# Feeding a recurrent attention loop by blocks: per-block rows instead of a resident copy, and second buffers for what is stored

## The chip, the cores and the metric

The kernel runs on one core of one Trainium2 chip. The time is device microseconds of one execution. Five engines work side by side and meet through semaphores: PE (TensorE: matrix products and transposes, into PSUM), DVE (VectorE), ACT (ScalarE), POOL (GpSimd) and SP (SyncE), which in this kernel issues every DMA, one after the other in one queue.

## What is computed

The reference is one layer's output and all its gradients. The layer adds to x a recurrent attention with memory and a dense block, both of the normalized x:

```python
def _A_ref(x, mem0, Wq, Wk, Wv, Wo, seg_len):          # x 1 x 2048 x 512, 32 heads of 128, seg_len 32
    mem = mem0                                          # 8 rows
    for s in range(n_seg):                              # 64 segments
        h = jnp.concatenate([mem, x[:, s*seg_len:(s+1)*seg_len]], axis=1)      # 40 rows
        q, k, v = (jnp.einsum('btd,dhe->bhte', h, W) for W in (Wq, Wk, Wv))
        p = _softmax(jnp.where(mask, jnp.einsum('bhqe,bhke->bhqk', q, k) * scale, -1e9))
        o = jnp.einsum('bhte,hed->btd', jnp.einsum('bhqk,bhke->bhqe', p, v), Wo)
        mem = o[:, :M]                                  # the first 8 rows go to the next segment
        outs.append(o[:, M:])
# out = x + _A_ref(xn, ...) + w2 @ relu(w1 xn + b1)**2 + b2 ; then the vjp by grad_out
```

What matters is that segment s + 1 can't begin before the eight memory rows of segment s are there.

## The kernel before

The program has seven stages, one after the other.

**Stage 1** (lines 181 to 329) works in four pieces of 512 rows: `norm` normalizes x, turns it on PE and keeps the result as `HT` (128 x 4 x 2048, channels on the partitions, all rows on the free axis). Then come the dense block forward and backward. Two "jobs" per 128 rows, 32 in this stage, turn weights for later: `wturn` reads a piece of a weight with a DMA transpose into `wtt` (line 245) and, three jobs later, stores it to DRAM as S_WOT or S_WT (line 249). The other 32 jobs are left over for stage 3.

**Stage 2** (331 to 376) forms the dense weights' gradients.

**Stage 3** (379 to 405) projects the rows that wait at the end of each segment. Each segment's window has 40 places, 8 for memory and 32 for its own rows; the kernel lays the sequence out so that a segment's 32 columns of `HT` are 8 memory rows and 24 of its own, and the first 8 of its own rows, which the memory displaces, are the "left" rows. `XL` gathers these from `HT` (line 386, three copies on DVE and one on ACT), 512 columns in all. 48 products `dNL` of 128 rows by 1024 follow, each of eight matrix multiplications (line 396), copied out of PSUM half by ACT and half by DVE (398) into one of six buffers, and stored to S_NL by one DMA (399). Wo, 4 MB, is loaded as the stage begins (382).

**Stage 4** (407 to 884) is the forward recurrence: 64 steps, grouped in 16 blocks of four. A step projects q, k and v from `HT` (427), copies them from PSUM into the tile `N` (411 ACT, 414 DVE; the profile calls it f_N), turns q and k on PE (166) and copies them back, forms scores, softmax, the weighted sums into the block's tile `OT`, gathers them through Wo (468), sums over groups (479, 487), and writes the eight memory rows of the next step into `HT` (414, "HT<-ps_sum"). Three stores save the step for the backward pass: `soN` (861: q and k rows out of N), `soV` (860: v rows out of N), `soP` (862: the probabilities, E). The left rows of block b are worked on during block b + 1, woven into its steps.

The order in this stage is written by hand: `F_ORDER` has one line for each of the four steps of a block, and `play` (582) issues the named pieces in just that order; a trailing "-" takes the piece of the step or block before, a "+" that of the one after, and "L." names left work. So each engine's queue, SP's too, has a fixed order. In it `soV` of the third step stands in the fourth, behind four other transfers of left work, and `soV` of the fourth stands in the next block's first step. `N` has one buffer: the first copy of a step waits until the step before has stored all of it.

`OT` has one buffer as well. When a block is done, `sO` (698) stores it to DRAM as S_OB, and during the next block four DMA transposes `t0` to `t3` (702) read it from there into `OC` (two buffers, one tag with `ON`), which `u0` to `u3` (704) store as S_ON. `otr` (747) turns the left rows' sums, OTL, straight out of SBUF into ON; `lo` (752) stores that. `sx` (761, 762) stores the block's output and its piece of `HT`.

**Stages 5 to 7** go backward over the left rows, backward over the 64 steps, and form the attention weights' gradients from what was stored.

In stages 1 to 3 a scheduler of the language orders each engine's instructions; in stage 4 and in the backward loop the written order stands.

Of the kernel before, what the change touches and what calls it, by code (L numbers as in the profile page):

```python
# [12 lines left out]
P = 128  # L13
# [13 lines left out]
def kernel(  # L27
# [74 lines left out]
    HG = 4  # L102
# [14 lines left out]
    S_HT = dram.tile([P, DC, S], BF16, name="S_HT")  # L117
    S_GM = dram.tile([P, DC, S], BF16, name="S_GM")
# [15 lines left out]
    S_OB = dram.tile([NB, P, HG, KH, P], BF16, name="S_OB")  # L134
# [46 lines left out]
    with sb("p1", 1) as p1, sb("p1b", 2) as p1b:  # L181
# [6 lines left out]
        def norm(rb):  # L188

            x = xq[rb]  # L190
            bs_ = p1b.tile([P, RCB, 6], F32, name="bs_", tag="bs_")
            mv = p1b.tile([P, RCB, 2], F32, name="mv", tag="mv")
            for c in range(RCB):
                nc.vector.bn_stats(bs_[:, c, :], x[:, c, :])
                nc.vector.bn_aggr(mv[:, c, :], bs_[:, c, :])
            veps = p1b.tile([P, RCB], F32, name="veps", tag="veps")
            nc.vector.tensor_scalar(out=veps[:], in0=mv[:, :, 1], scalar1=EPS, scalar2=None, op0=ALU.add)
            nc.scalar.sqrt(veps[:], veps[:])
            nc.vector.reciprocal(rstd_t[:, rb * RCB:(rb + 1) * RCB], veps[:])
            xn = p1b.tile([P, RCB, D], BF16, name="xn", tag="xn")  # L200
            for c in range(RCB):
                nc.vector.tensor_scalar(out=xn[:, c, :], in0=x[:, c, :], scalar1=mv[:, c, 0:1],
                                        scalar2=rstd_t[:, rb * RCB + c:rb * RCB + c + 1], op0=ALU.subtract,
                                        op1=ALU.mult)
# [55 lines left out]
        for rb in range(NRB):  # L260
# [68 lines left out]
        dma(out_8.rearrange("(c p) -> p c", p=P), gb1b[:])  # L329

# [52 lines left out]
    with sb("fl", 2) as fl:  # L383
        XL = fl.tile([P, DC, NB * NL], BF16, name="XL", bufs=1)
        for dc in range(DC):
            nc.any.tensor_copy(XL[:, dc].rearrange("p (s t) -> p s t", t=M),
                               HT[:, dc].rearrange("p (s r) -> p s r", r=SEG)[:, :, 0:M])
        for t in (1, 0, 2):
            for g in range(HG):
                for q in range(NB // 4):  # L390
# [8 lines left out]
                    dma(S_NL[4 * q:4 * q + 4, 32 * g:32 * g + 32, t, :], dN[:])  # L399
# [182 lines left out]
    def play(order, n, steps, lefts, step, blk, last={}):  # L582
# [36 lines left out]
    with sb("fw", 1) as fw, psum("fr", 4) as fr, psum("fpp", 1) as fpp, \  # L619
# [42 lines left out]
        nc.vector.tensor_copy(HT[:, :, 0:M], psm0[:, 0:DC * M].rearrange("p (c m) -> p c m", c=DC))  # L662
# [21 lines left out]
        def left(b):  # L684
# [13 lines left out]
            o["sO"] = lambda: dma(S_OB[b], B_["OT"][:].rearrange("p g k j r -> p g k (j r)"))  # L698
            for g in range(HG):
                def tO(g=g):  # L700
                    st["OC", g] = fo.tile([P, KH, P], BF16, name="OC", tag="OC", bufs=2)
                    nc.sync.dma_start_transpose(st["OC", g][:], S_OB[b][:, g].rearrange("p k r -> p (k r)"))
# [57 lines left out]
            def sx():  # L760
                dma(out0flat[b * P:(b + 1) * P, :], B_["bb"][:])
                dma(S_HT[:, :, b * P:(b + 1) * P], HT[:, :, b * P:(b + 1) * P])
            o["sx"] = sx
            return o

        def fwd(s):
# [3 lines left out]
            hT = HT[:, :, s * SEG:(s + 1) * SEG]  # L770
            shapes = {"kT": (fo, [P, KH, HG, L]), "qT": (fo, [P, KH, HG, SEG]), "N": (fo, [P, 3, GW])}
# [26 lines left out]
            for t, u, n in ((1, 2, "k"), (0, 1, "q"), (2, 0, "v")):  # L798
                for p in range(2):
                    def mm(n=n, p=p, t=t):  # L800
                        ps[n, p] = big("ps_proj")
                        proj(ps[n, p], hT, Wqkv, t * HD, p)
# [51 lines left out]
            def HTf():  # L854
                if s + 1 < NSEG:
                    ENGS["HT"](HT[:, :, (s + 1) * SEG:(s + 1) * SEG + M], st["sum"][:, :, 0:M])
# [11 lines left out]
        def load_back():  # L868
# [5 lines left out]
            dma(back["WoT"][:], S_WOT[:])  # L874
        with tc.manual_schedule():
# [9 lines left out]
    ht_cm.__exit__(None, None, None)  # L885
# [501 lines left out]
```

## Time and profile before

| | |
|---|---|
| median of 3 runs | 3427.52 us (3426.79 to 3429.24) |
| the profiled execution, its span | 3435.4 us |
| PE busy | 2761.0 us, 80% |
| DVE, ACT, POOL busy | 1220.0, 1017.2, 187.6 us |
| packets under 512 B | 650689 of 881602 |
| DMA engines' mean busy share | 74.8% in SP's queue |

The profiled execution's own time is its span, 7.9 us (0.23%) above the median of the runs. In the views, "A <- B" means that A came when B let it; times are microseconds from the start of the span, and "x3" counts instructions that a row merges. A row of SP's queue has how long SP was held by issuing that DMA, not how long the transfer took; a row "DMA a<-b" of the chain of waits has issue to landing. "PEclk" is the granted share of PE's clock.

### The profile page before, as it was taken

Reading aid. Unit: us, or ns where it says so; the run is one execution under the profiler, and the core shown is the slowest. Engines: PE = TensorE matmul, PEld = TensorE weight load, DVE = VectorE, ACT = ScalarE, POOL = GpSimd, SP = SyncE. Lnnn points to the kernel's source line nnn. Section 1 sums busy time; section 2 is a strip of 40 time slices with the busy share of each in tenths; the row PEclk is TensorE's granted clock in tenths of the full one; section 3 lists DMA queues with packets and bytes.
Section 4 is the critical chain, followed back from the end, with each engine's and each line's share of the span. In section 5 each row is a group of like instructions: output and inputs, shape, how many; then the busy total and the mean of one; then the engine's idle time right before and its main releaser. Section 6 shows DMA issues by size and latency. Waiting matters only on the chain.

```text
span 3435.4 us, 115446 instructions
## 1 busy us (share of the span) xinstructions
PE 2761.0 (80%) x51768; PEld 1351.9 (39%) x51768; DVE 1220.0 (36%) x3529; ACT 1017.2 (30%) x2493; POOL 187.6 (5%) x329
## 2 busy tenths in 40 slices
PE   7998854788777888774558888888788865999999
PEld 3453322444344444442233444344344432444444
DVE  5440112555454554542334444344444420010101
ACT  2331111333343343331333334333333320111111
POOL 0000001000000000000000000000000000000000
PEclk9999987999999999996679999999999988999999
DMA  9948997566657656667975767766766779999992
GB/s 259 269 116 333 217 174 132 146 163 168 174 156 181 173 164 181 161 173 220 257 202 151 204 162 181 190 163 171 199 158 172 206 201 224 224 194 226 190 196 77
DMA packets 881602, 644.73 MB, mean 188 GB/s; under 512 B 650689, under 2 KB 737362, under 8 KB 869714
## 3 DMA queue, kind: packets, MB, share of 16 engines
q1 hardware_dynamic: 881106, 637.34, 74.8%
q8 instruction: 406, 6.65, 0.8%
q14 instruction: 90, 0.74, 0.1%
HBM read 224.54 MB, written 264.25 MB: 142 GB/s over the span
## 4 chain that ended last, share of the span: by engine, by line
PE 58%; DMA 16%; SPq 11%; DVE 5%; ACT 5%; issue 4%; ACTq 0%; POOLq 0%; POOL 0%; DVEq 0%
PE ps_gw L1348 15%; PE ps_gR L468 11%; PE ps_proj L427 8%; SPq L245 3%; PE b_pp L553 3%; DMA S_A<-f_N 3%; PE ps_tr L166 3%; DMA S_GOL<-l_gON 3%; PE ps_R L468 3%; DMA ON<-OTL 2%; ACT R L411 2%; PE ps_sum L479 2%; PE ps_RL L1055 1%; PE ps_w L354 1%; DMA b_qN<-S_A 1%
## 5 line engine op out<-in xcount | busy, mean ns | idle before, releaser
L1348 PE MATMUL ps_gw<-gn,HNc 128*128 128x512 bf16 x1920 | 416.4, 379 | 0.0
L427 PE MATMUL ps_proj<-Wqkv,HT 128*32 128x512 bf16 x6144 | 378.8, 398 | 18.2 <-DVE HT L414 17.9
L411 ACT CAST f_N<-ps_proj 128x512 bf16<-128x512 f32 x320 | 182.1, 585 | 376.7 <-DMA S_A<-f_N 197.2
L1348 PEld LDWEIGHTS <-HNc 128*128 128x128 bf16 x1920 | 187.8, 98 | 223.9
L427 PEld LDWEIGHTS <-HT 128*32 128x32 bf16 x6144 | 161.1, 101 | 186.9 <-DVE HT L414 30.0
L1323 ACT CAST wt<-ps_gw 128x512 bf16<-128x512 f32 x126 | 70.7, 589 | 514.2 <-PE ps_gw L1348 291.9
L1306 DVE TENSOR_TENSOR gx<-ps_rows,gb 128x512 f32<-128x512 f32 x16 | 11.1, 692 | 495.7 <-PE ps_rows L1304 465.1
L1348 PE MATMUL ps_gw<-GOc,gn 128*128 128x512 bf16 x640 | 142.8, 386 | 18.9 <-DMA gn<-S_ON 18.9
L468 PE MATMUL ps_gR<-WT,b_gq 128*32 128x512 bf16 x2048 | 148.8, 406 | 7.6 <-issue 7.5
L468 PE MATMUL ps_gR<-WT,b_gk 128*32 128x512 bf16 x2048 | 148.4, 409 | 7.6 <-issue 7.5
L468 PE MATMUL ps_gR<-WT,b_gv 128*32 128x512 bf16 x2048 | 142.4, 391 | 5.6 <-issue 5.4
L396 PE MATMUL ps_L<-Wqkv,XL 128*128 128x512 bf16 x384 | 98.8, 410 | 57.1 <-ACT dNL L398 56.1
L166 PE MATMUL ps_tr<-ident,f_N 128*128 128x128 bf16 x1024 | 85.7, 234 | 70.2 <-ACT f_N L411 68.4
L427 PE MATMUL ps_proj<-WoT,GT 128*32 128x512 bf16 x2048 | 123.9, 384 | 22.3 <-DVE GT L414 18.0
L468 PE MATMUL ps_R<-Wo,OT 128*32 128x512 bf16 x2048 | 126.5, 389 | 1.1 <-issue 1.1
L1129 POOL COPY b_vT<-b_vl 128x1024 bf16<-128x1024 bf16 x64 | 66.6, 1041 | 911.9 <-PE ps_sc L448 476.4
L414 DVE CAST f_N<-ps_proj 128x512 bf16<-128x512 f32 x64 | 44.3, 692 | 196.8 <-DMA S_A<-f_N 147.8
L479 PE MATMUL ps_sum<-R,sel 128*32 128x128 f32 x1152 | 63.2, 293 | 60.7 <-ACT R L411 55.4
L411 ACT CAST gON<-ps_proj 128x512 bf16<-128x512 f32 x128 | 74.9, 585 | 116.7 <-PE ps_proj L427 112.9
L166 PEld LDWEIGHTS <-f_N 128*128 128x128 bf16 x1024 | 63.3, 104 | 109.6 <-ACT f_N L411 98.9
L1348 PEld LDWEIGHTS <-gn 128*128 128x128 bf16 x640 | 63.6, 99 | 96.8 <-DMA gn<-S_ON 19.2
L411 ACT CAST b_gq<-b_pp 128x256 bf16<-128x256 f32 x128 | 47.6, 372 | 160.5 <-PE b_pp L553 151.6
(215 smaller groups left out, 4415.0 us busy)
## 6 DMA issues: line engine op xcount, KB each, us to landing
S_A<-f_N SPq DMA_DIRECT2D x64, 512.0 KB
out_dram<-wt SPq DMA_DIRECT2D x154, 128.0 KB
S_A<-f_N SPq DMA_DIRECT2D x64, 256.0 KB
S_OB<-OT SPq DMA_DIRECT2D x16, 1024.0 KB
S_ON<-OC SPq DMA_DIRECT2D x64, 256.0 KB
b_qN<-S_A SPq DMA_DIRECT2D x64, 256.0 KB
b_kN<-S_A SPq DMA_DIRECT2D x64, 256.0 KB
S_GB<-b_gv SPq DMA_DIRECT2D x16, 1024.0 KB
```

Of the source, the lines that this page charges most:

```text
L166: nc.tensor.transpose(ps_ap, in_ap, ident[base:base + k, base:base + k])
L245: nc.sync.dma_start_transpose(wt[:], src)
L396: nc.tensor.matmul(ps[:], lhsT=XL[:, dc, q * P:(q + 1) * P], rhs=Wqkv[:, dc, c0:c0 + 512], start=(dc == 0), stop=(dc == DC - 1))
L411: nc.scalar.copy(out, in_)
L414: nc.vector.tensor_copy(out, in_)
L427: nc.tensor.matmul(ps[32 * g:32 * g + 32, :], lhsT=hT[:, dc, :], rhs=W[:, dc, c:c + 4 * P], start=(dc == 0), stop=(dc == DC - 1), tile_pos ...
L468: nc.tensor.matmul(R[32 * g:32 * g + 32, :], lhsT=XT(k, g), rhs=W[:, g * KH + k, :], start=(first and k == 4 * h), stop=(last and k == 4 * ...
L479: nc.tensor.matmul(ps["n"][SEG * c:SEG * c + SEG, 0:P], lhsT=sel[:], rhs=R4()[:, c * P:(c + 1) * P], start=True, stop=True, tile_position= ...
L553: nc.tensor.matmul(o, lhsT=N_[32 * g:32 * g + m, kk * P:(kk + 1) * P], rhs=X(kk)[32 * g:32 * g + m], start=(i == 0), stop=(i == len(jobs) ...
L1129: nc.gpsimd.tensor_copy(vT[:, :, :, 0:SEG], C["vl"][:])
L1323: nc.any.tensor_copy(wt[:], ps[:])
L1348: nc.tensor.matmul(ps[:], lhsT=l(rc), rhs=r(rc), start=(n == 0), stop=(n == RC_ALL - 1))
```

## The change

1. `HT` lives only in stage 1. `norm` also stores each 128 columns of it to DRAM (S_HX, 16 stores of 128 x 4 x 128). The left rows are gathered at the end of stage 1 by 16 small copies on POOL into `xl`, stored (S_XL), and `XL` of stage 3 is loaded from there.
2. The columns of `XL` have another order: within 128 of them, the block is now the fastest index and not the slowest. The store to S_NL is written accordingly: `rearrange("b r c -> r b c")`. The bytes and where they go are the same.
3. In stage 4 each block has a tile `X` (two buffers), loaded by `hl` from S_HX a block ahead; projections read it, the memory rows are written into it, and `hs` stores it to S_HT in the block's last step, where `sx` did it two blocks later.
4. `N` and `OT` have two buffers. `sO` and S_OB are gone: `t0` to `t3` turn `OT` straight from SBUF.

```diff
+    S_HX = dram.tile([S // P, P, DC, P], BF16, name="S_HX")
+    S_XL = dram.tile([P, DC, S // SEG * M], BF16, name="S_XL")
-    S_OB = dram.tile([NB, P, HG, KH, P], BF16, name="S_OB")
...
+            for c in range(RCB):
+                b0 = rb * RB + c * P
+                dma(S_HX[b0 // P], HT[:, :, b0:b0 + P])
...
+                xl = p1.tile([P, DC, NB * NL], BF16, name="xl")
+                for dc in range(DC):
+                    for q in range(NB // SPB):
+                        nc.gpsimd.tensor_copy(
+                            xl[:, dc, q * P:(q + 1) * P].rearrange("p (j t b) -> p b j t", t=M, b=SPB),
+                            HT[:, dc].rearrange("p (q b j r) -> p q b j r", b=SPB, j=SPB, r=SEG)[:, q, :, :, 0:M])
+                dma(S_XL[:], xl[:])
...
-        for dc in range(DC):
-            nc.any.tensor_copy(XL[:, dc].rearrange("p (s t) -> p s t", t=M),
-                               HT[:, dc].rearrange("p (s r) -> p s r", r=SEG)[:, :, 0:M])
+        dma(XL[:], S_XL[:])
...
-                    dma(S_NL[4 * q:4 * q + 4, 32 * g:32 * g + 32, t, :], dN[:])
+                    dma(S_NL[4 * q:4 * q + 4, 32 * g:32 * g + 32, t, :].rearrange("b r c -> r b c"), dN[:])
...
-        "k0mm L.pm1 q1mm q0mm ld k0ev xt- q1ev q0ev k1mm soV- k0fl q0fl L.tu1 k1ev k0Te q1fl q0Te k1fl k1Te s0 "
+        "k0mm L.hl++ L.pm1 q1mm q0mm ld k0ev xt- q1ev q0ev k1mm soV- k0fl q0fl L.tu1 k1ev k0Te q1fl q0Te k1fl k1Te s0 "
...
-                shapes = {"kL": (fs, [P, KH, HG, NL], BF16), "OT": (fo, [P, HG, KH, SPB, SEG], BF16),
+                shapes = {"kL": (fs, [P, KH, HG, NL], BF16), "OT": (fs, [P, HG, KH, SPB, SEG], BF16),
+                          "X": (fs, [P, DC, P], BF16),
...
-            o["sO"] = lambda: dma(S_OB[b], B_["OT"][:].rearrange("p g k j r -> p g k (j r)"))
-                    nc.sync.dma_start_transpose(st["OC", g][:], S_OB[b][:, g].rearrange("p k r -> p (k r)"))
+                    nc.sync.dma_start_transpose(st["OC", g][:], B_["OT"][:, g].rearrange("p k j r -> p (k j r)"))
...
-                dma(S_HT[:, :, b * P:(b + 1) * P], HT[:, :, b * P:(b + 1) * P])
+                    dma(B_["X"][:], S_HX[b])
+            o["hs"] = lambda: dma(S_HT[:, :, b * P:(b + 1) * P], B_["X"][:])
...
-            shapes = {"kT": (fo, [P, KH, HG, L]), "qT": (fo, [P, KH, HG, SEG]), "N": (fo, [P, 3, GW])}
+            shapes = {"kT": (fo, [P, KH, HG, L]), "qT": (fo, [P, KH, HG, SEG]), "N": (fs, [P, 3, GW])}
```

Tiles of the pool `fo` have one buffer, those of `fs` two. `L.sO` is gone from the first line of F_ORDER, and `L.hs+` stands in the fourth, right behind its first two pieces.

Where instructions moved. First, SP's queue at the start of stage 3; wtt is a turned piece of a weight. Before:

```order
L382 DMA Wo<-in_A_Wo_dram 128x32x512
L399 DMA S_NL<-dNL 4x32x1024 x2
L245 DMA_TRANSPOSE wtt<-in_A_Wk_dram 128x2x512
L399 DMA S_NL<-dNL 4x32x1024
L245 DMA_TRANSPOSE wtt<-in_A_Wk_dram 128x2x512
L399 DMA S_NL<-dNL 4x32x1024
```

And now:

```order
L394 DMA Wo<-in_A_Wo_dram 128x32x512
L397 DMA XL<-S_XL 128x2048
L249 DMA_TRANSPOSE wtt<-in_A_Wk_dram 128x2x512 x4
L253 DMA S_WT<-wtt 128x1024
L249 DMA_TRANSPOSE wtt<-in_A_Wk_dram 128x2x512
L253 DMA S_WT<-wtt 128x1024
L249 DMA_TRANSPOSE wtt<-in_A_Wk_dram 128x2x512
L409 DMA S_NL<-dNL 32x4x1024
```

The load of XL stands behind that of Wo, four transposes have moved ahead of the first store, and the store's shape begins with 32 where it began with 4.

Second, SP's queue in the second half of a block in stage 4, from the store of the third step's probabilities to that of the fourth step's q and k. Before:

```order
L862 DMA S_A<-E 128x512
L783 DMA f_vLs<-S_NL 104x1024
L861 DMA S_A<-f_N 128x2048
L704 DMA S_ON<-OC 128x1024
L747 DMA_TRANSPOSE ON<-OTL 128x8x128
L751 DMA S_PL<-EL 128x512
L752 DMA S_OL<-ON 128x1024
L860 DMA S_A<-f_N 128x1024
L702 DMA_TRANSPOSE OC<-S_OB 128x8x128
L706 DMA_TRANSPOSE vTM<-vM 128x8x128
L754 DMA bb<-S_B 128x512
L861 DMA S_A<-f_N 128x2048
```

And now:

```order
L876 DMA S_A<-E 128x512
L796 DMA f_vLs<-S_NL 104x1024
L875 DMA S_A<-f_N 128x2048
L777 DMA S_HT<-X 512x1x128
L713 DMA S_ON<-OC 128x1024
L756 DMA_TRANSPOSE ON<-OTL 128x8x128
L760 DMA S_PL<-EL 128x512
L761 DMA S_OL<-ON 128x1024
L874 DMA S_A<-f_N 128x1024
L711 DMA_TRANSPOSE OC<-OT 128x8x128
L715 DMA_TRANSPOSE vTM<-vM 128x8x128
L763 DMA bb<-S_B 128x512
```

The store of X has come in ahead of the store of OC; the transpose of OC reads OT.

Third, DVE in stage 1, where the second piece's rows xn are normalized; bs__936 and bs__945 are the statistics of the third piece. Before:

```order
L197 TENSOR_SCALAR veps<-mv 128x4
L194 BN_STATS bs__936<-xq 128x6
L277 SCALAR_TENSOR_TENSOR gh1T,gb_142<-ps_ga,rT 128x512
L199 RECIPROCAL rstd_t<-veps 128x4
L195 BN_AGGR mv<-bs__936 128x2
L194 BN_STATS bs__936<-xq 128x6
L202 TENSOR_SCALAR xn<-xq,mv,rstd_t 128x512 x4
```

And now:

```order
L198 TENSOR_SCALAR veps<-mv 128x4
L281 SCALAR_TENSOR_TENSOR gh1T,gb_143<-ps_ga,rT 128x512
L200 RECIPROCAL rstd_t<-veps 128x4
L203 TENSOR_SCALAR xn<-xq,mv,rstd_t 128x512 x4
L195 BN_STATS bs__945<-xq 128x6
```

The third piece's statistics, which need its load, have moved behind the second piece's rows. PE's instructions stand in the same order as before from end to end; only the names of what they read differ.

More of the change, by code (lines that the diff above doesn't have):

```diff
@@ L329 @@
         dma(out_8.rearrange("(c p) -> p c", p=P), gb1b[:])
+    ht_cm.__exit__(None, None, None)
     wq_cm = None
@@ L761, in sx, with hl @@
                 dma(out0flat[b * P:(b + 1) * P, :], B_["bb"][:])
-                dma(S_HT[:, :, b * P:(b + 1) * P], HT[:, :, b * P:(b + 1) * P])
             o["sx"] = sx
+            def hl():
+                if b > 0:
+                    dma(B_["X"][:], S_HX[b])
+            o["hl"] = hl
+            o["hs"] = lambda: dma(S_HT[:, :, b * P:(b + 1) * P], B_["X"][:])
             return o
@@ L801, in mm @@
                         ps[n, p] = big("ps_proj")
-                        proj(ps[n, p], hT, Wqkv, t * HD, p)
+                        proj(ps[n, p], B_["X"][:, :, j * SEG:(j + 1) * SEG], Wqkv, t * HD, p)
                     o["%s%dmm" % (n, p)] = mm
@@ L855, in HTf @@
                 if s + 1 < NSEG:
-                    ENGS["HT"](HT[:, :, (s + 1) * SEG:(s + 1) * SEG + M], st["sum"][:, :, 0:M])
+                    b1, j1 = divmod(s + 1, SPB)
+                    ENGS["HT"](block(b1)["X"][:, :, j1 * SEG:j1 * SEG + M], st["sum"][:, :, 0:M])
             o["HT"] = HTf
@@ L874, in load_back @@
             dma(back["WoT"][:], S_WOT[:])
+        X0 = block(0)["X"]
+        dma(X0[:], S_HX[0])
+        nc.vector.tensor_copy(X0[:, :, 0:M], psm0[:, 0:DC * M].rearrange("p (c m) -> p c m", c=DC))
         with tc.manual_schedule():
@@ L884 @@
     wo_cm.__exit__(None, None, None)
-    ht_cm.__exit__(None, None, None)
     bw_cm, bw, WoT = back["cm"], back["bw"], back["WoT"]
```

2 lines of the change are left out of this document (removed), and 4 rows, old and new, of the table F_ORDER.

## The prediction

> **What bounds the kernel now.** I read the time by stages first, then the waits in total, then the chain of waits inside one block of the forward loop, and last SP's queue in stage 3. The table of stretches gives for each its length, the busy time of PE, PEld, DVE, ACT and POOL, PE's granted clock, the DMA engines' share and GB/s; these are stage 2, stage 3 and the loop of stage 4:
>
> ```profile
> 272.00:375.00 103.00, 102.41 (x496) 48.50 (x496) 2.36 (x5) 14.29 (x29) 0.00 (x0) 0.98 0.79 306
> 375.00:564.00 189.00, 99.05 (x388) 39.75 (x388) 34.13 (x55) 28.62 (x50) 6.67 (x30) 0.86 1.15 180
> 564.00:1557.00 993.00, 791.54 (x18710) 411.16 (x18709) 500.72 (x1568) 375.71 (x824) 51.29 (x128) 0.95 0.62 164
> ```
>
> Stage 2 is PE's own (102.41 of 103 us). Stage 3 isn't: PE has 99 us of work in 189, the DMA engines are fuller than in stage 2 and move only 180 GB/s instead of 306. In the loop PE idles 201 of 993 us. The waits in total, as microseconds, times, longest:
>
> ```profile
> ACT f_N L411 <- DMA S_A<-f_N: 197.2, 30, 7.9
> DVE f_N L414 <- DMA S_A<-f_N: 147.8, 34, 6.1
> ACT dNL L398 <- DMA S_NL<-dNL: 112.7, 33, 6.1
> PE ps_tr L166 <- ACT f_N L411: 68.4, 42, 3.4
> PE ps_L L396 <- ACT dNL L398: 56.1, 35, 2.9
> ```
>
> In the loop the copies into N wait for the stores out of N, and PE, which wants to turn what is copied, waits 68.4 us for them. In stage 3 the copies into dNL wait for the stores to S_NL. The first two rows are long because those engines have little else to do; only the fourth is on PE, and it is the one to price.
>
> The copies of the memory rows on DVE mark the steps of a block (start, duration):
>
> ```profile
> 896.26 0.19 DVE L414 CAST HT<-ps_sum 128x32 bf16<-128x32 f32 x1 [0.42 <-PE ps_sum L487]
> 909.70 0.19 DVE L414 CAST HT<-ps_sum 128x32 bf16<-128x32 f32 x1 [0.42 <-PE ps_sum L487]
> 923.34 0.19 DVE L414 CAST HT<-ps_sum 128x32 bf16<-128x32 f32 x1 [0.42 <-PE ps_sum L487]
> 940.01 0.19 DVE L414 CAST HT<-ps_sum 128x32 bf16<-128x32 f32 x1 [0.46 <-PE ps_sum L487]
> 958.34 0.19 DVE L414 CAST HT<-ps_sum 128x32 bf16<-128x32 f32 x1 [0.42 <-PE ps_sum L487]
> ```
>
> The steps last 13.44, 13.64, 16.67 and 18.33 us, 62.1 in all. The chain of waits, in the third of these, shows why it is long:
>
> ```profile
> 910.18 4.24 DMA S_ON<-OC
> ...
> 920.57 4.36 DMA ON<-OTL
> ...
> 925.35 2.50 DMA S_A<-f_N
> ...
> 928.00 1.57 ACT f_N L411 x3
> ...
> 929.62 0.41 PE ps_tr L166 x4
> ```
>
> The v rows of the third step are stored only at 925.35, because SP stood behind the transpose into ON; ACT copies the fourth step's rows from 928.00, and PE turns them at 929.62, more than six microseconds after that step began.
>
> **Part 1: second buffer for N, -66 us.** With two buffers the first copy of a step needs the stores of two steps ago. These were issued over a step, some 13 us, earlier, and land in 2.50 (row above) to 4.24 us (the same kind of store, S_ON). So the wait goes. What is late next is the flip's own input: a copy of q0 follows its projection by some 0.6 us, while PE still projects three more halves. The first two steps of the block already run like that. I take 66 of the 68.4 us: bounds 45 (if a third of the waits reappears elsewhere) and 70. Per block that is 4.2 us, 62.1 to 57.9.
>
> **Part 2: the store to S_NL, with XL loaded, -62 us.** SP's queue, stage 3, start and time held:
>
> ```profile
> 375.48 0.40 SPq L382 DMA_DIRECT2D Wo<-in_A_Wo_dram  x1
> ...
> 428.12 1.23 SPq L399 DMA_DIRECT2D S_NL<-dNL  x2
> 429.40 4.74 SPq L245 DMA_TRANSPOSE wtt<-in_A_Wk_dram  x1
> ...
> 435.48 2.65 SPq L245 DMA_TRANSPOSE wtt<-in_A_Wk_dram  x1
> ```
>
> A transpose behind two stores holds SP 4.74 us, one behind a single store 2.65: each store costs about 2 us more than its own row. The same instruction in stage 1 (Wq) and here (Wk), as least, median and most ns:
>
> ```profile
> L245 SPq DMA_TRANSPOSE wtt<-in_A_Wq_dram x16: 1277/1392/2431, 110.1 to 160.1; - x16
> L245 SPq DMA_TRANSPOSE wtt<-in_A_Wk_dram x16: 2451/3100/6002, 385.1 to 459.4; - x16
> ```
>
> The rows of the other two issues of the stage, of the eight matrix multiplications of a product, and of a store's landing:
>
> ```profile
> L399 SPq DMA_DIRECT2D S_NL<-dNL x48: 537/568/5244, 378.3 to 548.4; - x48
> ```
>
> ```profile
> L249 SPq DMA_DIRECT2D S_WT<-wtt x42: 430/571/1048, 119.7 to 543.8; - x42
> ```
>
> ```profile
> 395.08 1.89 PE L396 MATMUL ps_L<-Wqkv,XL 128*128 128x512 bf16 x8 [0.32 <-ACT dNL L398]
> ```
>
> ```profile
> 428.12 6.58 DMA S_NL<-dNL
> ```
>
> A store of 256 KB to S_NL lands in 6.58 us; S_ON, 256 KB too but with 128 as first dimension on both sides, in 4.24. Stage 1 turns and stores weights at 1392 + 571 ns each. What stage 3 has besides is the store with a shape that begins with 4. I therefore expect the form with 32 to hold SP for its 568 ns and no more. Then SP needs 48 x 0.568 + 32 x 1.392 + 32 x 0.571 = 90.1 us, PE 48 x 1.89 = 90.7. Two queues of the same length that wait for each other don't run at the pace of one: I take 104 us (2.17 a product). If transposes stay at 3.1, SP needs 27.3 + 99.2 + 18.3 = 144.8.
>
> The Trainium skill (DMA: Bandwidth & Descriptors, Rules for kernel authors) says that a DMA uses as many of the 16 engines as divide the slowest dimension of both its patterns, so a leading 4 confines it to four. By that rule the new store has sixteen, and as an estimate its 2 us fall to 0.5, which by itself would put this term near -65. No run shown here has the store in the new form.
>
> Against this stands the load of XL, which was 1 us of copies and now is a transfer behind the 4 MB of Wo. The nearest rows are a load of 4 MB (WoT) and the transfer issued behind it, issue and then landing:
>
> ```profile
> 1563.83 0.39 SPq L874 DMA_DIRECT2D WoT<-S_WOT  x1
> ```
>
> ```profile
> 1564.27 14.55 DMA OC<-S_OB
> ```
>
> So XL, issued at 375.93, lands at 390.5 (at 380.3, if it could pass, by the 4.36 of ON). PE idles until then and starts at a lower clock, 2 us as an estimate: 0.86 was granted over the idle-ridden stage 3, 0.98 over stage 2.
>
> The Trainium skill (the same page, Queues, rings and completion order) speaks against this edit: an engine takes a ring's descriptors in order, so XL can't pass Wo. By it the wait is paid in full, as I take it; if XL passed, this term would be -72.
>
> The end of the stage, the load of the first memory rows and the first projection:
>
> ```profile
> 554.65 9.05 DMA memN<-in_A_mem_dram
> ...
> 564.28 6.15 PE ps_proj L427 x64
> ```
>
> memN is queued behind the late stores; I take 5 us, between 2.5 (S_A above) and 9.05; X's first block comes in its shadow. So 390.5 + 2 + 104 + 0.6 + 5 + 0.5 = 502.6 instead of 564.3: -62. Best: 380.3, PE's 90.7 and 2.5 give -90; worst with transposes at 3.1 and memN at 9.05: 390.5 + 2 + 144.8 + 10 = 547, -17.
>
> **Part 3: stage 1, 16 stores more, -1 us.** These rows hold the price of a store of this shape, and the third ordering shown above:
>
> ```profile
> L762 SPq DMA_DIRECT2D S_HT<-HT x16: 598/619/1109, 724.4 to 1597.3; - x16
> ```
>
> ```profile
> 45.88 0.69 DVE L194 BATCH_NORM_STATS2 bs__936<-xq 128x6 f32<-128x512 bf16 x1 [3.90 <-DMA xq<-in_A_x_dram]
> ...
> 47.82 1.36 DVE L202 TENSOR_SCALAR xn<-xq,mv,rstd_t 128x512 bf16<-128x512 bf16 x4
> ```
>
> ```profile
> 48.27 0.40 PE L166 MATMUL ps_tr<-ident,xn 128*128 128x128 bf16 x2 [9.45 <-DVE xn L202]
> ```
>
> PE's 9.45 us of idling ended late because DVE first waited 3.90 us for the third piece's load; that load's statistics now stand behind xn, so 3.9 + 0.7 us come back. Twelve of the stores fall where SP is on the chain: 12 x 0.62 = 7.4 us, of which PE, ahead of its stores by two buffers, should see half. Together -1; bounds -5 and +8. The gathering on POOL is hidden: POOL is idle in this stage. So is S_XL's store, needed 100 us later.
>
> **Part 4: blocks and OT, 0 us.** `hl` is two steps ahead of its use. The projections read X as they read HT. `sO` removes a 1 MB store, `t0` to `t3` read from SBUF:
>
> ```profile
> L747 SPq DMA_TRANSPOSE ON<-OTL x16: 1262/2028/3449, 667.0 to 1587.4; - x16
> ```
>
> ```profile
> L702 SPq DMA_TRANSPOSE OC<-S_OB x64: 1231/1297/8007, 652.8 to 1590.8; - x64
> ```
>
> Issued from SBUF a transpose of this size holds SP 0.7 us longer, 2.9 a block. `hs` waits in SP's queue for the last memory rows of its block, and `u1`, `otr`, `lo`, `soV`, `t0` stand behind it:
>
> ```profile
> 919.77 0.42 SPq L704 DMA_DIRECT2D S_ON<-OC  x1
> ```
>
> `u1` was issued here and now waits until after 923.34: 3.6 us a block. Who waits for that? The soV behind it, which now has a whole step to land; the loads after it are needed in the next step. So nothing, as long as SP catches up within the step; without that cover up to 2.9 + 3.6 = 6.5 us a block.
>
> **Sum.** -66 - 62 - 1 = -129 against the profiled execution's 3435.4: 3306. It stands 7.9 us above the median, 3427.5, so the median would be 3298.
>
> **The rivals.** *A, the store's form doesn't matter* (what is slow is the amount, not the shape): stage 3 is then as long as now, 173 us from first product to last store, and starts 15 + 2 us late; +17 - 66 - 1 = -50, 3377. For it: no run shows the new form. Against it: 6.58 to 4.24, and stage 2's 306 GB/s. *B, the wait moves*: SP's 6.5 us are only partly caught up, and PE, rid of the wait for f_N, waits for f_vLs, the load behind `soN` in the next step. At half of part 1, 2.1 us in each of 15.5 blocks, 33 us are lost: 3331. For it: SP's queue is what made the old wait. Against it: that load hangs on soN, which hangs on the copies, which come sooner. *C, slower: SP becomes the loop's bound.* If each of four transposes takes the 3449 of the row above instead of 1297, SP loses 8.6 us a block, with `hs` 12.2, and nothing in the order lets it catch up: 15.5 x 12.2 = 189 us against 129 gained, 3488. It decides from 8.3 us a block on (129 / 15.5). Against it: SP waits for other engines in every step, which is slack.
>
> **How the numbers follow.** Forecast 0.78, A 0.08, B 0.09, C 0.03, and 0.02 for an unforeseen sum near nothing. A measurement of this kernel tells about 0.2%, 7 us, from no change. The forecast's own range is 3265 (part 2 at -90, part 1 at -70) to 3345 (one of the two at its worst bound: -17 or -45); B lies in it. A and C are left out. Faster 0.95, same 0.02, slower 0.03.
>
> **What would show it.** Right: no wait of f_N for S_A in the list; blocks of 57 to 59 us with the third and fourth step near 15; transposes of stage 3 near 1.4 us and the first projection near 500; the first matrix multiplication of stage 3 near 390, behind a wait for XL. Wrong: transposes still at 3 us (A); waits for f_vLs or SP held at `hs` past a step (B, C); a second wait that ends at PE's turns.

## The result and the profile after

The changed kernel takes 3267.6 us (median of 4 runs, 3253.2 to 3272.1) where the kernel before takes 3428.4 (4 runs, 3426.8 to 3431.7): a ratio of 0.951, 95% interval 0.948 to 0.954 (the two medians alone give 0.953). That is 161 us less by the medians; the forecast was 130. By the ratio it is 0.951 x 3427.5 = 3260, just beyond the fast end of the forecast's range, 3265. The profiled execution has a span of 3266.8 us against 3435.4, so 168.6 us are to be explained, where the prediction summed up 129.

The table of stretches, cut at the same events in both kernels: end of stage 2, first projection of the forward loop, its last projection, first product of the backward loop, first product of the weight gradients, end. Before (the columns are length, busy time of PE, PEld, DVE, ACT and POOL, PE's granted clock, DMA share, GB/s):

```profile
0.00:374.60 374.60, 334.56 (x1904) 168.01 (x1904) 123.90 (x301) 96.56 (x140) 3.35 (x10) 0.96 0.81 244
374.60:564.30 189.70, 99.08 (x392) 39.77 (x395) 34.70 (x57) 28.97 (x50) 6.67 (x30) 0.86 1.15 180
564.30:1550.30 986.00, 787.09 (x18559) 408.93 (x18563) 497.13 (x1559) 373.48 (x819) 51.29 (x128) 0.95 0.62 164
1550.30:1785.20 234.90, 109.74 (x3081) 60.54 (x3077) 74.60 (x189) 59.10 (x145) 1.50 (x3) 0.65 0.86 237
1785.20:2827.50 1042.30, 866.25 (x25229) 415.45 (x25229) 434.63 (x1344) 382.38 (x1181) 87.86 (x126) 0.96 0.69 177
2827.50:3435.40 607.90, 564.27 (x2624) 259.17 (x2624) 55.07 (x82) 76.70 (x158) 36.93 (x32) 0.96 0.89 192
```

And after:

```profile
0.00:370.10 370.10, 330.41 (x1869) 167.12 (x1904) 122.42 (x302) 96.22 (x140) 8.67 (x26) 0.97 0.86 254
370.10:488.80 118.70, 85.05 (x381) 38.19 (x388) 33.42 (x51) 28.52 (x49) 6.70 (x30) 0.88 1.05 291
488.80:1379.80 891.00, 756.04 (x18559) 399.70 (x18563) 499.56 (x1562) 376.78 (x819) 51.54 (x128) 0.99 0.66 166
1379.80:1609.90 230.10, 106.46 (x3080) 59.34 (x3076) 75.01 (x190) 59.47 (x147) 1.51 (x3) 0.67 0.90 242
1609.90:2649.20 1039.30, 862.26 (x25229) 415.04 (x25228) 434.92 (x1342) 382.35 (x1181) 88.28 (x126) 0.96 0.69 177
2649.20:3266.80 617.60, 563.96 (x2572) 259.53 (x2624) 55.07 (x82) 73.71 (x158) 36.99 (x32) 0.96 0.96 190
```

| stretch | forecast | measured |
|---|---|---|
| stages 1 and 2 | -1 | -4.5 |
| stage 3 | -62 | -71.0 |
| forward loop (its blocks) | -66 | -95.0 |
| tail, left rows backward | 0 | -4.8 |
| backward loop | 0 | -3.0 |
| weight gradients | 0 | +9.7 |
| sum | -129 | -168.6 |

Three rows matter. The loop gave 29 us more than its term. Its idle time fell from 986.0 - 787.1 = 198.9 us to 891.0 - 756.0 = 135.0, by 64, which is the term; but PE also spends 31 us less on the same 18559 instructions, at a clock of 0.99 instead of 0.95. Stage 3 gave 9 us more. And the last stage, which nobody touched, became 10 us longer.

PE's waits in the loop after, longest first; the row of the flips that waited for f_N (68.4 us before) isn't among them, and no wait of that size has taken its place:

```profile
PE ps_sum L489 <- ACT R L421: 38.2, 54, 0.7
PE ps_sum L497 <- DVE F L424: 19.9, 48, 0.4
PE f_pp L563 <- DVE OT L424: 19.3, 34, 0.6
PE f_pp L563 <- DVE ET L471: 18.2, 35, 1.2
PE ps_proj L437 <- DVE X L424: 17.9, 63, 0.3
PE f_pp L563 <- DMA f_vLs<-S_NL: 6.7, 8, 1.7
```

The memory rows mark a block, now written into X:

```profile
895.47 0.19 DVE L424 CAST X<-ps_sum 128x32 bf16<-128x32 f32 x1 [0.42 <-PE ps_sum L497]
908.97 0.19 DVE L424 CAST X<-ps_sum 128x32 bf16<-128x32 f32 x1 [0.42 <-PE ps_sum L497]
922.66 0.19 DVE L424 CAST X<-ps_sum 128x32 bf16<-128x32 f32 x1 [0.42 <-PE ps_sum L497]
936.28 0.19 DVE L424 CAST X<-ps_sum 128x32 bf16<-128x32 f32 x1 [0.46 <-PE ps_sum L497]
950.23 0.19 DVE L424 CAST X<-ps_sum 128x32 bf16<-128x32 f32 x1 [0.42 <-PE ps_sum L497]
```

The steps last 13.50, 13.69, 13.62 and 13.95 us, 54.8 together, instead of 13.44, 13.64, 16.67 and 18.33: the third and fourth are as short as the first two, not "near 15". In stage 3 the transposes hold SP for 1.4 us (least, median, most), as forecast, and the first product waits for XL:

```profile
L249 SPq DMA_TRANSPOSE wtt<-in_A_Wk_dram x16: 1286/1434/3567, 379.7 to 425.2; - x16
L249 SPq DMA_TRANSPOSE wtt<-in_A_Wv_dram x16: 1335/1404/2161, 428.6 to 478.1; - x16
```

```profile
386.90 0.61 PE L406 MATMUL ps_L<-Wqkv,XL 128*128 128x512 bf16 x1 [16.80 <-DMA XL<-S_XL]
```

### The profile page after: what moved, and what is told of

Read it like the earlier page. It is cut to its first block, busy times and chain, and to the rows that moved or that the text cites. A ratio compares the mean times of both kernels' runs of the same rounds, so it can differ in the third digit from the quotient of the medians.

```text
span 3266.8 us, 115469 instructions
## 1 busy us (share of the span) xinstructions
PE 2704.2 (83%) x51673; PEld 1338.9 (41%) x51768; DVE 1220.4 (37%) x3526; ACT 1017.1 (31%) x2492; POOL 193.7 (6%) x345
## 4 chain that ended last, share of the span: by engine, by line
PE 57%; DMA 13%; SPq 13%; DVE 7%; issue 5%; ACT 5%; ACTq 0%; POOLq 0%; POOL 0%; DVEq 0%
PE ps_gR L478 11%; PE ps_proj L437 11%; PE ps_gw L1364 8%; SPq L1289 6%; PE b_pp L563 3%; PE ps_R L478 3%; DMA S_GOL<-l_gON 3%; PE ps_tr L167 2%; ACT R L421 2%; PE ps_sum L489 2%; PE ps_L L406 2%; DMA out_dram<-wt 2%; PE ps_w L366 2%; PE ps_w L386 1%; PE ps_RL L1071 1%
## 5 line engine op out<-in xcount | busy, mean ns | idle before, releaser
L437 PE MATMUL ps_proj<-Wqkv,X 128*32 128x512 bf16 x6144 | 361.9, 385 | 18.2 <-DVE X L424 17.9
L437 PEld LDWEIGHTS <-X 128*32 128x32 bf16 x6144 | 156.9, 98 | 174.7 <-DVE X L424 29.9
L406 PE MATMUL ps_L<-Wqkv,XL 128*128 128x512 bf16 x376 | 84.8, 385 | 18.2 <-DMA XL<-S_XL 16.8
L421 ACT CAST b_gk<-b_pp 128x256 bf16<-128x256 f32 x128 | 47.8, 373 | 150.7 <-PE b_pp L563 115.5
L424 DVE CAST b_gq<-b_pp 128x256 bf16<-128x256 f32 x128 | 54.4, 425 | 107.0 <-PE b_pp L563 102.8
L437 PEld LDWEIGHTS <-GT 128*32 128x32 bf16 x2048 | 49.5, 98 | 78.4 <-DVE GT L424 30.0
```

Of the source, the lines that this page charges most:

```text
L406: nc.tensor.matmul(ps[:], lhsT=XL[:, dc, q * P:(q + 1) * P], rhs=Wqkv[:, dc, c0:c0 + 512], start=(dc == 0), stop=(dc == DC - 1))
L421: nc.scalar.copy(out, in_)
L437: nc.tensor.matmul(ps[32 * g:32 * g + 32, :], lhsT=hT[:, dc, :], rhs=W[:, dc, c:c + 4 * P], start=(dc == 0), stop=(dc == DC - 1), tile_pos ...
```

## Experiments

The theory with which they began: the wait for N costs its idle time and, on top, the lower clock of the multiplications behind it; stage 3 gained by the store's form; part 4 is worth nothing. The runs were made on other chips, where the kernel before took 3447 to 3449 us, so times are compared by their ratio to the kernel before on the same chip, and stages by the profiles.

### N without a wait and without memory (v_apart)

```diff
-... "N": (fo, [P, 3, GW])}
+... "N": (fo, [P, 2, GW]), "V": (fo, [P, GW])}
```

(and the v rows are copied into V, read and stored from it)

> The kernel before, with one edit: the v rows of a step get a tile of their own beside that of the q and k rows, each with one buffer, so no memory is added and nothing else of the change is made. Theory (the wait for N cost its idle time and, on top, a lower clock in the matrix multiplications that follow it): the copies of q then wait only for the store of the q and k rows, which is issued some 6 us before that of the v rows, so the waits go as with two buffers. PE idles 64 us less in the forward loop and is busy 31 us less there, its granted clock rises from 0.95 to 0.99: 3428 - 95 = about 3333. Rival 1 (the wait cost its idle time alone, and the other 29 us come from the X tile, the weighted sums turned from SBUF or the missing store to S_OB): busy time stays at 787 us, 3428 - 64 = about 3364. Rival 2 (the store of q and k is itself late): part of the waits stays, 3390 or more.

Ratio 0.974 (0.972 to 0.977). The loop of this kernel:

```profile
565.60:1462.40 896.80, 756.50 (x18559) 400.15 (x18563) 499.36 (x1557) 376.61 (x819) 51.38 (x128) 0.99 0.69 180
```

It is 89.2 us shorter than before, busy 756.5, clock 0.99. So 89 of the loop's 95 us are the wait for N, with all that follows it; X and the turning from SBUF aren't needed for the drop of the busy time. And the second buffer wasn't needed for it: what the copies of q and k waited for was the store of v rows that they share a tile with.

### N with a wait in the changed kernel (n_single_again)

```diff
-... "N": (fs, [P, 3, GW])}
+... "N": (fo, [P, 3, GW])}
```

> The kernel after, with N back in a single buffer; all else of the change stays. Theory (wait plus lower clock, both N's): the forward loop is 986 us again, busy 787, clock 0.95: 3268 + 95 = about 3363. Rival 1 (N's part is the idle time alone, the rest is the other edits'): 3268 + 66 = about 3334, with PE's busy time still at 756 us in the loop.

Ratio 0.994 (0.992 to 0.997), worse than both expected; the loop, and its longest wait:

```profile
491.60:1523.10 1031.50, 793.79 (x18559) 416.16 (x18563) 499.89 (x1566) 373.50 (x819) 51.23 (x128) 0.93 0.55 145
```

```profile
PE ps_tr L167 <- ACT f_N L421: 108.9, 41, 6.0
```

The wait is 108.9 us instead of 68.4, and the loop 45.5 us longer than in the kernel before. The rest of the change delays the store of v rows further: `hs`, which waits for the block's last memory rows, stands ahead of it in SP's queue. The steps fit this: the third of a block, in which `hs` is issued, lasts 20.1 us in the mean instead of 17.1, the fourth 17.6 as before. The second buffer hides that. Against the changed kernel the loop is 140.5 us longer: 108.9 of wait, 37.8 of busy time for the same instructions, less 6.2 of other idle time.

### The form of the store alone (store_new)

```diff
-... XL[:, dc].rearrange("p (s t) -> p s t", t=M), HT[:, dc].rearrange("p (s r) -> p s r", r=SEG)[:, :, 0:M]
+... XL[:, dc, q * P:(q + 1) * P].rearrange("p (j t b) -> p b j t", t=M, b=SPB), ...
-dma(S_NL[4 * q:4 * q + 4, 32 * g:32 * g + 32, t, :], dN[:])
+dma(S_NL[4 * q:4 * q + 4, 32 * g:32 * g + 32, t, :].rearrange("b r c -> r b c"), dN[:])
```

> The kernel before, with the new form of the store to S_NL alone: XL is still copied from the resident HT, its columns in the order that lets the store begin with 32 rows. Theory (the form makes the transposes and the store slow; the load of XL behind Wo gives back 15 us of it in the changed kernel): stage 3 from its first product to the first projection 189 - 86 = about 103 us, transposes near 1.39 us, 3428 - 86 = about 3342. Rival A of the prediction (the amount, not the shape, is slow, and the changed kernel gained elsewhere in this stage): no change, 3428.

Ratio 0.979 (0.976 to 0.982). Stage 3 and the loop:

```profile
381.70:499.80 118.10, 86.18 (x385) 37.46 (x396) 35.44 (x64) 30.26 (x55) 6.67 (x30) 0.95 1.03 289
499.80:1485.80 986.00, 787.19 (x18559) 409.93 (x18563) 497.69 (x1562) 373.58 (x819) 51.34 (x128) 0.95 0.62 165
```

Rival A falls: the form alone takes 71.6 us off stage 3. But the theory falls too in one point. This kernel has XL at once, and its stage 3 is no shorter than that of the changed one (118.7), which waits 16.8 us for XL. So the wait seems to cost nothing, and something else to hold both at 118; the next two runs look for it.

### XL ahead of Wo (xl_first)

```diff
+        dma(XL[:], S_XL[:])
         dma(Wo[:], A_Wo.rearrange("h e d -> e h d"))
-        dma(XL[:], S_XL[:])
```

> The kernel after, with the load of XL issued ahead of that of Wo. The prediction charged the wait for XL with 14.55 us and added the products behind it. Theory now (the DMA engines are full through the whole stage, share 1.00 to 1.09 in each stretch of it, so the order of two loads changes nothing): the first product starts 12 us earlier, at about 375, and the first projection at 489 as before; stage 3 118 us, no change in time. Rival (the prediction's sum, wait plus products): stage 3 106 to 108 us, 11 us faster than the changed kernel.

Ratio 0.955 (0.953 to 0.958); the changed kernel had 0.951 (0.948 to 0.954). The first product starts 5.1 us after stage 2 instead of 16.8, and the stage doesn't change:

```profile
374.90:493.40 118.50, 87.80 (x388) 38.18 (x388) 33.41 (x51) 28.51 (x49) 6.67 (x30) 0.92 1.03 291
```

In the same stage of the changed kernel, cut in pieces, the DMA engines are busy throughout, also in the last piece, in which PE is done and waits for what is queued. The share alone doesn't show that they are the bound, since it was 1.15 in the kernel before with only 180 GB/s; the next run tests it.

```profile
387.00:400.00 13.00, 12.78 (x50) 5.46 (x52) 3.83 (x6) 3.52 (x6) 0.00 (x0) 0.83 1.03 268
400.00:440.00 40.00, 39.79 (x183) 18.09 (x185) 15.54 (x23) 12.91 (x22) 0.00 (x0) 1.00 1.09 285
440.00:475.00 35.00, 32.11 (x146) 14.36 (x147) 12.20 (x18) 10.42 (x18) 1.67 (x8) 1.00 1.07 290
475.00:488.80 13.80, 0.26 (x4) 0.18 (x4) 1.85 (x6) 1.30 (x3) 5.03 (x23) 0.56 1.00 318
```

### Wo in stage 2 (wo_early)

```diff
+    wo_cm = sb("wo", 1)
+    wop = wo_cm.__enter__()
+    Wo = wop.tile([P, H, D], BF16, name="Wo")
     with sb("p2", 1) as p2:
...
             dma(Wqkv[:, :, t * HD:(t + 1) * HD], ...)
+        dma(Wo[:], A_Wo.rearrange("h e d -> e h d"))
...
-    wo_cm = sb("wo", 1)
-    wop = wo_cm.__enter__()
-    Wo = wop.tile([P, H, D], BF16, name="Wo")
-    dma(Wo[:], A_Wo.rearrange("h e d -> e h d"))
```

> The kernel after, with Wo's memory set aside before stage 2 and its 4 MB loaded right behind Wqkv, in a stretch of stage 2 where the DMA engines are busy 0.26 of the time (355 to 371 us) and PE is the bound. If the DMA engines bound stage 3, it loses 4.19 MB at 290 GB/s, 14 us: stage 3 about 104 us, the time 14 us below that of the changed kernel, about 0.947 of the kernel before. Rival (stage 3 is bound by SP's queue): no more than 4 us are saved. Should the stores of stage 2's results be held up by the load, stage 2 grows from 103 us and takes some of it back.

Ratio 0.952 (0.949 to 0.955), no different from the changed kernel. Stages 2 and 3:

```profile
271.10:378.70 107.60, 105.28 (x496) 49.17 (x496) 1.97 (x3) 13.63 (x27) 0.00 (x0) 0.96 0.88 331
378.70:486.80 108.10, 86.48 (x392) 38.45 (x396) 33.76 (x52) 28.52 (x49) 6.67 (x30) 0.91 1.04 282
```

Taking 4 MB away shortens stage 3 by 10.6 us: near the estimate of 14 for a stage bound by DMA, and more than the 4 that a stage bound by SP's queue would give. But stage 2 takes 107.6 us where the changed kernel takes 102.8 (267.3 to 370.1), so 6 us are left.

### Work in the wait, and a delay without a wait (fill_wait, pad_no_wait)

```diff
 def fl_(n=n, p=p, u=u):
+    if (n, p) == ("q", 0) and j in (0, 3):
+        pad = fpp.tile([P, 2, 512], F32, name="pad", tag="pp0")
+        for _ in range(8):
+            nc.tensor.matmul(pad[:, 0, :], lhsT=ident[:], rhs=Wqkv[:, 0, 0:512], start=True, stop=True)
```

In fill_wait this stands in the kernel before; in pad_no_wait, with 10 instead of 8, in v_apart, where nothing waits at this place.

> The kernel before, with work added: ahead of the first turn of the q rows in the third and fourth orderings' steps (j = 0 and j = 3), where PE waits about 2.2 us, PE does eight matrix multiplications of 128x512 whose result nobody reads, about 1.7 to 1.9 us; the wait itself, its buffers and all else stay. Theory (a wait costs a lower clock afterwards): the waits become shorter than a microsecond, the low clock behind them goes, 31 us of busy time are saved at most and about 5 us are lost in the steps whose wait is shorter than the filling: about 3405, faster than before although it does more. Rival 1 (no such effect): the filling hides in the wait, the few short waits cost 5 us, about 3433.

> The kernel before with the v rows in a tile of their own (no wait for N), and with work in the place where the wait was: ten matrix multiplications of 128x512 that nobody reads ahead of the first turn of the q rows in the steps j = 0 and j = 3, about 2.3 us, which is as long as the wait was, but with PE at work. Without the filling the forward loop is 896.8 us, with the wait it was 986. Theory (a wait costs more than its length since a lower clock follows it): 31 x 2.3 = 71 us are added, the loop is about 968 us, its clock 0.98 or more, and the 18 us that are missing to 986 are the price of the lower clock. Rival (a delay at this place costs more than its own length through the copies behind it, and the clock costs nothing): 986 or more.

Ratios: 0.999 (0.997 to 1.001) and 0.993 (0.991 to 0.995, beside 0.974 for v_apart). The loop of fill_wait and what is left of its wait; then the loop of pad_no_wait:

```profile
569.60:1551.50 981.90, 815.54 (x18783) 422.71 (x18819) 494.00 (x1558) 371.27 (x819) 51.40 (x128) 0.98 0.62 165
```

```profile
PE ps_tr L166 <- ACT f_N L411: 13.9, 27, 1.8
```

```profile
569.10:1521.90 952.80, 814.42 (x18879) 428.43 (x18883) 496.06 (x1557) 374.21 (x819) 51.77 (x128) 0.99 0.65 170
```

The two answer different questions. **pad_no_wait**: its fillings hold PE for 2.17 us each, 69.4 in all, as long as the waits of the kernel before (68.4). They cost 952.8 - 896.8 = 56 us (theory: 71), the waits cost 89. So the same delay is 33 us dearer in this loop where PE waits than where it works (theory: 18). Of these, 21 are what a wait costs beyond its length, and 13 what the fillings cost less than theirs: PE's waits for the loads of f_vLs and vM, 11.5 us in v_apart, don't occur behind them.

**fill_wait**: with PE at work the clock is 0.98, and all but the filling (53.6 us of recorded busy time) takes 762 us instead of 787, so the wait does bring the low clock. But the loop is only 4 us shorter, where the theory had about 25. PE idles 22 us more apart from the wait for f_N (981.9 - 815.5 - 13.9 = 152.5, before 198.9 - 68.4 = 130.5); some 7 of the 22 are the eighth multiplication of each filling, of which the trace has seven. The filling and what is left of the wait are 53.6 + 7 + 13.9 = 74.5 us, 6 more than the wait was, so the better clock returned 4 + 6 = 10 of its 25 us. The other 15 PE waits elsewhere, for the probabilities ET and for the loads of f_vLs and of vM (4.8 us instead of 0.9). Before, and then with the filling:

```profile
PE f_pp L553 <- DVE ET L461: 10.2, 24, 2.0
```

```profile
PE f_pp L553 <- DVE ET L461: 16.4, 34, 2.1
PE f_pp L553 <- DMA f_vLs<-S_NL: 9.3, 9, 1.7
```

v_apart has these waits too (18.8, 6.8 and 4.7 us), so a PE at the low clock seems to have covered them. Its 89.2 us are 68.4 of wait and 30.6 of busy time, less 9.8 of other waits that have appeared.

Is it the low clock that makes a wait cost more than its length, or do the copies of q and k, which are late in either case, delay something else? Steps of the kernel before with the wait but without slow multiplications tell the two apart. Compared with the mean of the same step of a block in the changed kernel, the 24 steps that have both, with 57.4 us of wait, last 84.2 us longer (two of them also wait for f_vLs, 1.4 and 1.8 us). The five with a wait alone have 8.9 us of wait and last 10.1 longer, 1.1 of it in one idle stretch that no wait in the trace explains (936.56, below). So the excess stands where the clock was low, and late copies by themselves cost about the wait's length. Five steps are few, and no run has early copies with a low clock.

### Both edits alone (two_edits)

Edit: those of v_apart and store_new together.

> The kernel before with two edits together, and nothing else of the change: the v rows of a step in a tile of their own (one buffer each), and the new form of the store to S_NL with XL copied from the resident HT. Each alone took off, in its own profile, 89 us in the forward loop and 72 us in stage 3. Theory (these two waits are all that the change gains): they add, forward loop 897 us, stage 3 118 us, 161 us less than before, a ratio of about 0.953, within 10 us of the changed kernel. Rival (the X tile, the turning from SBUF or the two stores and loads that replace the resident copy gain something too): more than 15 us behind the changed kernel.

Ratio 0.954 (0.951 to 0.956), against 0.951 (0.948 to 0.954) of the changed kernel in the result above and 0.954 (0.950 to 0.958) in a repetition (after_again, below). The two edits add, and reach about what the whole change reaches: forward loop 900.9 us, stage 3 118.8. Any advantage of the rest is too small to tell from the times.

### S_OB back (sob_again), and the place in HBM (same_place)

```diff
+    S_OB = dram.tile([NB, P, HG, KH, P], BF16, name="S_OB")
...
+            o["sO"] = lambda: dma(S_OB[b], B_["OT"][:].rearrange("p g k j r -> p g k (j r)"))
-                    nc.sync.dma_start_transpose(st["OC", g][:], B_["OT"][:, g].rearrange("p k j r -> p (k j r)"))
+                    nc.sync.dma_start_transpose(st["OC", g][:], S_OB[b][:, g].rearrange("p k r -> p (k r)"))
```

> The kernel after, unchanged, as a measure for the runs beside it on the same chip: about 0.951 of the kernel before, weight gradients about 617 us from their first product to the end.

> The kernel after, with part 4's main edit undone: the weighted sums of a block are stored to S_OB again (a 1 MB store a block) and turned from there. The prediction priced this edit at 0 in the loop. Theory: forward loop within 5 us of 891, the time within 7 us of the changed kernel. Rival 1 (the missing store and load were worth something): the loop is some 10 us longer. Rival 2 (turning from SBUF costs SP 2.9 us a block that show): the loop is shorter.

after_again: 0.954 (0.950 to 0.958), loop 898.1 us, weight gradients 621.1. sob_again: 0.964 (0.960 to 0.968), loop 930.3 us. Rival 1, and three times what it said. The rows of S_OB's transposes and, in the changed kernel, of those from SBUF, then a wait of sob_again's loop:

```profile
L713 SPq DMA_TRANSPOSE OC<-S_OB x64: 1231/1296/8633, 572.8 to 1466.4; - x64
```

```profile
L711 SPq DMA_TRANSPOSE OC<-OT x64: 1232/1299/7896, 569.8 to 1417.5; - x64
```

```profile
PE f_pp L564 <- DMA f_vLs<-S_NL: 23.8, 15, 2.8
```

A transpose holds SP for 1.30 us wherever it reads from. What costs is this wait, 23.8 us (10.9 in after_again). SP's queue and the chain, in one block of sob_again:

```profile
943.73 0.63 SPq L779 DMA_DIRECT2D S_HT<-X  x1
...
957.00 0.39 SPq L709 DMA_DIRECT2D S_OB<-OT  x1
```

```profile
962.11 5.45 DMA f_vLs<-S_NL
```

`hs` holds the queue until the memory rows of 943.7 are there; what stands behind it moves back, `sO` too, and its 1 MB goes out 5.1 us ahead of the load of f_vLs, which lands late. In two_edits, with `sO` but without `hs`, the same store goes out 8.1 us ahead (948.10 and 956.24), and the wait is 5.8 us. Over the blocks the lead is 4.3 to 8.2 us with `hs`, 8.1 to 10.6 without; that `hs` is the cause is read from these rows, as no run moves it alone. So this is rival B's wait, in a kernel that lacks one edit of the change. And again 13 us more of waiting cost 32, with 15 us more of busy time for the same instructions (772.8 against 757.9).

```diff
-    S_HX = dram.tile([S // P, P, DC, P], BF16, name="S_HX")
-    S_XL = dram.tile([P, DC, S // SEG * M], BF16, name="S_XL")
+    S_OB = dram.tile([8, S // P * P * DC * P], BF16, name="S_OB")
+    S_HX = S_OB[0].rearrange("(s p c q) -> s p c q", p=P, c=DC, q=P)
+    S_XL = S_OB[1, 0:P * DC * (S // SEG * M)].rearrange("(p c n) -> p c n", p=P, c=DC)
```

> The kernel after, with the scratch tensors in HBM laid out so that S_GB and S_GL lie at the addresses that they have in the kernel before (S_HX and S_XL become parts of a 16 MB tensor that takes the place of S_OB); no instruction is added, removed or moved. In the last stage, the weight gradients, the changed kernel takes 617.6 us against 607.9, on another chip 624 and 627 against 608, though nothing there was edited; its packets of 256 bytes, those of the transposes out of S_GB, take 28.1 ns in the mean against 24.2. Theory (the tensors' place in HBM sets these packets' time): 24 to 25 ns, the stage about 608 us, the time 10 to 15 us below that of the changed kernel. Rival (something else in the stage): 617 to 625 us, no change.

Ratio 0.949 (0.945 to 0.953). The last stage, in after_again and in same_place:

```profile
2653.40:3274.50 621.10, 567.06 (x2624) 259.75 (x2624) 55.05 (x82) 73.53 (x158) 36.92 (x32) 0.96 0.94 188
```

```profile
2657.40:3264.70 607.30, 563.21 (x2624) 258.99 (x2624) 55.08 (x82) 76.65 (x158) 36.92 (x32) 0.96 0.88 192
```

The 10 us are back. The trace's packets of 256 bytes in this stage take 23.6 ns in the mean, 27.1 in after_again (28.1 in the changed kernel's profile, 24.2 before). In time the two differ by 0.5%, which their intervals don't separate; the stage does, in every profile: 607 to 610 us in the eight kernels with S_GB at its old address, 613 to 630 in the six others; the packets' means are 23.5 to 24.2 and 26.6 to 28.1 ns. The addresses follow from the order in which the tensors are declared; the trace doesn't show them.

### The kernel that beats both (wo_place)

Edit: those of wo_early and same_place together.

> The kernel after, with both edits that may gain beyond it: Wo loaded in stage 2 behind Wqkv, and S_GB and S_GL at their old addresses. Stage 3 about 108 us, stage 2 some 5 us longer, weight gradients about 608 if the place is what costs there: 15 to 20 us less than the changed kernel, about 0.946 of the kernel before; if the place doesn't matter, 5 us less.

Ratio 0.946 (0.943 to 0.950): 3257.7 us (3253.9 to 3265.4) where after_again takes 3286.0 (3276.3 to 3298.1) and the kernel before 3447.9. Stage 3 takes 107.2 us, the weight gradients 608.1.

## Why the prediction was right or wrong

**Direction and causes: right.** The two waits that it named, for the stores out of N and for the stores to S_NL, are the change's gain; two_edits shows that they reach it by themselves. Of the signs named, these came: no wait for f_N, transposes at 1.4 us, a first product that waits for XL (386.9, forecast 390). These went further than said: blocks of 54.8 us and not 57 to 59, a first projection at 488.8 and not near 500.

**Part 1: mechanism right, size wrong; here most of the miss lies.** The step that failed is "I take 66 of the 68.4 us". It priced a wait at its idle time, and that was right for the idle time: -64. But the loop became 95 us shorter, 89 of them by N alone. The bound of 70 failed for the same reason: it was the wait row and nothing else. What it put at nothing, without a reason, is PE's busy time: 787.1 us before, 756.0 after, 31 less for the same instructions. Its sign stood in the prediction's own table, the loop's granted clock of 0.95: 787.1 us at 0.95 would be 755 at 0.99. The rows around a wait show where it arises. The 32 multiplications behind the wait of 2.85 us that ends at 946.75 take 2.97 us, those behind the wait of 1.42, in the step before, 1.90:

```profile
930.65 1.90 PE L427 MATMUL ps_proj<-Wqkv,HT 128*32 128x512 bf16 x32
...
949.54 2.97 PE L427 MATMUL ps_proj<-Wqkv,HT 128*32 128x512 bf16 x32
```

```profile
944.00:948.00 4.00, 1.02 (x12) 0.67 (x12) 1.86 (x6) 1.86 (x4) 0.00 (x0) 1.00 0.02 4
948.00:952.00 4.00, 3.98 (x74) 2.06 (x78) 3.61 (x14) 1.90 (x5) 0.80 (x2) 0.57 0.79 257
```

The clock's price can't be had back by the clock alone: with work in the wait 25 of the 31 us went and only 10 showed in the loop, since a faster PE then stands at other waits (fill_wait). The step of the wait of 1.42 has no slow multiplication and yet lasts 16.67 us, where the same step of the changed kernel lasts 13.62; besides its wait it holds an idle stretch of PE that occurs once in the loop:

```profile
936.56 1.47 PE L468 MATMUL ps_R<-Wo,OT 128*32 128x512 bf16 x22 [1.10 <-issue]
```

**Part 2: size nearly right, working wrong.** -71.0 instead of -62. The transposes and the store did what was said. What failed is the sum "390.5 + 2 + 104": it put the wait for XL and the products one behind the other, as if PE and SP were the stage's bound. They aren't: the DMA engines are, once the store no longer slows them (wo_early), and whether PE starts at 380 or 387 is the same (xl_first). The products took 86 us in the changed kernel, not 104; where they begin early they take longer, 97 in xl_first and 101 in store_new. The Trainium skill's rule on the slowest dimension (DMA: Bandwidth & Descriptors, Rules for kernel authors) would make this term -65 by the prediction's estimate; the stage went from 180 to 291 GB/s, which agrees with it in direction.

**Part 3: -4.5 instead of -1** for stages 1 and 2, within its bounds of -5 and +8. No run tests it alone, and its size is uncertain: stage 2 ends at 374.6 to 381.7 us in the six profiles that have stages 1 and 2 of the kernel before, at 370.1 to 374.9 in the six that have those of the changed kernel.

**Part 4: 0 was nearly right for the sum, and wrong in its parts.** The loop has 891 and 898 us in two profiles of the changed kernel, 897 in v_apart. The transposes from SBUF were priced 0.7 us too high, by a row (ON<-OTL) that had something else in it: its median is 2.03 us before and 1.32 in the changed kernel. `hs` was said to cost nothing as long as SP catches up. That holds only with the covers of this change: without the second buffer of N the loop is 45 us longer than before (n_single_again), 2.9 us a block, inside the 6.5 given; with `sO` still in the queue it is 32 us longer than in the changed kernel (sob_again).

**The rivals.** A fell (store_new). B's wait is in the changed kernel with 6.7 us, and with 23.8 where `sO` stays. C fell: SP's median transpose stayed at 1.30 us.

**Nothing in the prediction** had the +9.7 us of the last stage: removing S_OB and adding two scratch tensors moved S_GB in HBM (same_place).

## What to carry to other kernels

Price a wait by the difference between a step that has it and one that hasn't, not by the row of the wait: here 68 us of waiting were worth 89. Ask of a buffer that is waited for which part of it is still in use; parting a tile can do what doubling it does, for no memory. Before summing a wait and the work behind it, look whether the DMA engines are full in that stage: if they are, moving a wait inside the stage may gain nothing, as here, where fewer bytes and another form of the transfers did.

## What was not expected of the hardware

- The clock fell in steps whose longest wait was 1.2 to 3.4 us. Of 29 steps before with a wait of 0.94 to 3.42 us at the flips, 24 have projections or gatherings of over 550 ns each (380 at full clock), of the 62 steps of the changed kernel 6. In the trace's record the granted clock stood at one half for 3.41 us at a time, in 23 of 25 falls (twice longer): 95.5 us of the loop before, 20.5 after. The Trainium skill (TensorE: Matmul & The Clock Gate, Part 1) gives one idle window of about 3.4 us as what lowers the clock; here the shortest wait in a step with slow ones is 1.23 us, and two of over 1.9 us are in steps without.
- Where a scratch tensor lies in HBM changed the mean time of 256-byte packets from 27.1 to 23.6 ns, and a stage of 621 us by 14, with the same instructions (after_again, same_place).
- A DMA transpose of 256 KB holds SP for 1.30 us in the median whether it reads SBUF or HBM.
